# An attention and Fourier-mixing kernel on one Trainium2 core: sine table taken in during the first loads, last 64 rows in two column halves, a new instruction order

## The chip, the cores and the metric

The kernel runs on one core of a Trainium2 chip. The core has a matrix engine (TensorE, in the profile PE, its weight loads PEld), a vector engine (VectorE, DVE), an engine for activation functions (ScalarE, ACT), a general engine (GpSimd, POOL), a fifth that here only issues transfers (SyncE, SP), and 16 DMA engines that carry out all transfers. Each engine works through its own instructions strictly in order; semaphores hold an instruction back until what it needs is there. SP, ACT and POOL each issue transfers from their own queue. The metric is the time of one execution on the device in microseconds (us), lower is better; the median of several runs counts.

## What is computed

`B, H, S, D = 8, 8, 576, 64`; features `F = 128`; `C = H*D = 512`; hidden width 2048. Cut to what matters:

```python
def phi(x):
    proj = einsum('bhsd,df->bhsf', x, w_phi)
    proj = proj - max(abs(proj), axis=-1)
    return concatenate([exp(proj), exp(-proj)], -1)
q_p, k_p = phi(q), phi(k)
num = einsum('bhsf,bhfd->bhsd', q_p, einsum('bhsf,bhsd->bhfd', k_p, v))
den = einsum('bhsf,bhf->bhs', q_p, sum(k_p, axis=2))[..., None] + 1e-06
x = num / den                        # (batch, seq, 512) after merging the heads
u = x + real(fft(fft(x, axis=seq), axis=channel))
un = (u - mean(u)) / sqrt(var(u) + 1e-06)
out = u + maximum(un @ w_ch1, 0) @ w_ch2
```

## The kernel before

The eight batches pass one after the other through the same chain, and several batches are in flight at once. Rows of a batch are cut into five tiles, called c = 0 to 4: four of 128 rows and c = 4 with the last 64 (rows 257 to 319 and row 0). For the first batch everything is loaded as float32 by SP's queue and turned by TensorE (`turn_first_k`, `turn_first_q`, line 346); later batches are loaded in bfloat16 by POOL's queue (line 256) and turned by DMA transposes on SP's queue (lines 380 to 394).

The steps of one batch, with the names of their PSUM tiles:

- keys `psk` (line 464, two halves of the four, `pj` pool of two buffers): ScalarE takes two exponentials of each (470), VectorE the maximum (484, `MK`); queries `psq` (520, maximum 528) and `psh`, `ph` (570, 549, exponentials 579, 554). The maxima give factors by which POOL scales v (`VCn`, `VCp`, lines 434 and 439) and `E` (536 to 543).
- heads: `kv` (660, 664, copied by ScalarE 668), `pn_` (675, combined by VectorE 682 to 689 and POOL 690 into `X`).
- mixing: the Fourier transform as matrix products with cosine and sine tables `CS, SS, CD, SD`: folds (622 to 636), `psD` (736), then three products `pu` (757), t = 0 and 1 each giving two row tiles and t = 2 giving c = 4; VectorE adds them to `X` (762 to 772).
- normalise: statistics and centring per row tile (785 to 794) in the order c = 0, 2, 1, 3, 4, each followed by a DMA transpose on SP's queue into `UT` (798).
- forward: `psf` (844, `UT` columns 0 to 287 first, which come from c = 0, 1, 2, then the others), ReLU by ScalarE (849), `pso` (856, for c = 4 line 871), added to `X` by VectorE (862, for c = 4 line 878), and stores on SP's queue (`store`, 816 to 825).

The tables are made once: VectorE reduces the arguments (167 to 213), ScalarE takes four sines (187, 193, 212, 216), POOL clears pads and mirrors halves (231 to 249). ScalarE needs a function table loaded for sine and another for the exponential; the compiler puts these loads (`ACT_TABLE_LOAD`) ahead of the first instruction that needs them.

What sets the order: the kernel is written as generators, one per step stream, and four strings of letters (`START`, `FIRST`, `PERIOD`, `LAST`) say which stream takes its next step. `weave` follows them, delaying a letter whose needs (`NEEDS`) or PSUM buffers (`TILES`) are not there. `PERIOD` is run five times. So the strings fix each engine's instruction order. The letter Z issues one matmul of `keep_warm` (831, tile `pz`), whose result nobody reads; there are 80. The `pz` tiles come from the same three `pb` buffers as `pst`, `psq`, `kv` of the first batch, `psf` and `pso`.

The end of the program: the last batch has nothing beside it. TensorE runs 128 matmuls of `psf`, 64 of `pso` and 16 of line 871; VectorE adds the two 64-row halves of the partial sum (878, twice); SP stores 63 rows (824) and row 0 (825).

Of the kernel before, what the change touches and what calls it, by code (L numbers as in the profile page):

```python
# [9 lines left out]
AT = mybir.ActivationFunctionType  # L10
ALU = mybir.AluOpType
AX = mybir.AxisListType
F32 = mybir.dt.float32
# [8 lines left out]
FIRST = "PTTTPMFFFMFTFPQMPTPTNFMFFFMFMTFFMTSPMRKTFFPFTMFFMTFFMTFMFFMFFFFPFMRMFBFFMFAFSFFSRTSFFFFFDTFFRFPTDFFRTFFMFFATFFNMFFMMFTPVMMTTNTFTFFFFFPFFTTFFPMFTFFPTTSFFPNNN"  # L22
PERIOD = "NFKFNMFFMFMFMFMFMRFMFMMMRFFFMFFMFMFFFPPFSFRFMFFFMTFPBMPFFFNPTFFDFFFFFTRFDPQTFFFTFFMFFTFMFPTFMMFTFVRFTMFFFFMFTTTFTSFFFSFFFFFNTSTFFSTFFNTTANM"
LAST = "TPMFFTFMFTFMFMFMFMSFMFMTFNNMMFFSMFTFMFFNFFMRFFMFFMFFMFTFFTDFTFPPFFRFSFFTFTTFFFRFFFDMTFRFSFMFMTRFSMMRMFMFRFFMFMFFFDTTMPPFTMMFFPFMATFNFKBFTKFFFMMFTFFTFFMFFFFFFFNFTFNMFBNMFFFFFTFTFTFPFPPTSFNFAFFMSFTFFTFTNMFMFQFFMFTFMFRMVFFMFFFTFTSNFFFFMTDFFTFMPFFSPMFSFRNFPFNFQFTFFFFFMVRFFFPTTFMFFP"

# [7 lines left out]
def kernel(  # L33
# [23 lines left out]
    const = ctx.enter_context(tc.tile_pool(name="const", bufs=1))  # L57
# [24 lines left out]
    W2b = const.tile([128, NHH, C], BF16, name="W2b")  # L82
# [29 lines left out]
    rc, rs = gc[:, 0:C], ga[:, 3 * NK:4 * NK]  # L112
# [187 lines left out]
    def load_first():  # L300
# [509 lines left out]
        yield  # L810


    def store(b, U, c):
        if c == 1:
            for a in range(8):
                nc.sync.dma_start(
                    out=out[b, 225 - 32 * a:257 - 32 * a, :].rearrange("(r j) n -> r j n", j=2),
                    in_=U[16 * a:16 * a + 16, 0:2, 0:C],
                )
        elif c in (2, 3):  # L820
            rows_ = out[b, 320:576, :].rearrange("(a r j) n -> a r j n", r=16, j=2)
            nc.sync.dma_start(out=rows_[:, ::-1, 3 - c, :], in_=U[:, c, 0:C])
        elif c == 4:
            nc.sync.dma_start(out=out[b, 257:320, :], in_=U[1:64, 4, 0:C])
            nc.sync.dma_start(out=out[b, 0:1, :], in_=U[0:1, 4, 0:C])


    def keep_warm(b):
# [8 lines left out]
    def forward(b):  # L837
        U, UT, rs = mixed[b]
        HT = fpool.tile([128, NHH, S], BF16, tag="HT", name="HT")
        for hf in range(2):  # L840
            for hh in range(NHH):
                ps = pb.tile([128, 288], F32, tag="pb", name="psf")
                for cc in range(NCC):
                    nc.tensor.matmul(  # L844
                        ps[:], lhsT=W1b[:, cc, 128 * hh:128 * hh + 128],
                        rhs=UT[:, cc, 288 * hf:288 * hf + 288],
                        start=(cc == 0), stop=(cc == NCC - 1),
                    )
# [19 lines left out]
        po = pb.tile([128, C], F32, tag="pb", name="pso")  # L868
        for hh in range(NHH):
            g = 64 * (hh % 2)  # L870
            nc.tensor.matmul(
                po[g:g + 64, :], lhsT=HT[:, hh, 512:576], rhs=W2b[:, hh, :],
                start=(hh < 2), stop=(hh >= NHH - 2),
            )
            if hh % 4 == 3 and hh < NHH - 1:
                yield
        for g in (0, 64):
            nc.vector.scalar_tensor_tensor(
                out=U[0:64, 4, 0:C], in0=po[g:g + 64, :], scalar=rs[0:64, 4:5],
                in1=U[0:64, 4, 0:C], op0=ALU.mult, op1=ALU.add,  # L880
            )
        store(b, U, 4)
        yield

# [43 lines left out]
    def fold_later(b):  # L928
# [64 lines left out]
        "F": lambda b, i: (  # L993
            [("pb", "F", i)] if i < 32
            else [("pb", "F", i + 7)] if i < 64 and i % 8 == 0
            else [("pb", "F", i + 3)] if i == 64 else []
        ),
    }
    BUFS = {"pj": 2, "pk": 1, "pb": 3}
# [75 lines left out]
```

## Time and profile before

| | us |
|---|---|
| median of 5 runs (444.71 to 448.17) | 446.13 |
| the profiled execution | 448.01 |
| its span, first to last instruction | 445.9 |
| TensorE busy | 413.3 |
| VectorE busy | 316.0 |
| ScalarE busy | 298.8 |
| GpSimd busy | 263.1 |

The profiled execution lies 2.1 us above its span, and its time is 1.9 us above the median of the runs. The five repeats of `PERIOD` can be seen in the chain of waits: it passes the same matmuls at 231.65, 279.54 and 327.43 us, so one repeat takes 47.89 us. In the tables of stretches a row gives, for each engine, busy us and in brackets the number of instructions, then the clock that TensorE was granted (1 is full) and the mean busy share of the DMA engines.

### The profile page before, as it was taken

Reading aid. Unit: us, or ns where it says so; the run is one execution under the profiler, and the core shown is the slowest. Engines: PE = TensorE matmul, PEld = TensorE weight load, DVE = VectorE, ACT = ScalarE, POOL = GpSimd, SP = SyncE. Lnnn points to the kernel's source line nnn. Section 1 sums busy time; section 2 is a strip of 40 time slices with the busy share of each in tenths; the row PEclk is TensorE's granted clock in tenths of the full one; section 3 lists DMA queues with packets and bytes.
Section 4 is the critical chain, followed back from the end, with each engine's and each line's share of the span. In section 5 each row is a group of like instructions: output and inputs, shape, how many; then the busy total and the mean of one; then the engine's idle time right before and its main releaser. Section 6 shows DMA issues by size and latency. Waiting matters only on the chain.

```text
span 445.9 us, 10240 instructions
## 1 busy us (share of the span) xinstructions
PE 413.3 (93%) x4021; PEld 254.5 (57%) x4044; DVE 316.0 (71%) x599; ACT 298.8 (67%) x617; POOL 263.1 (59%) x363
## 2 busy tenths in 40 slices
PE   3887888999997999999999999999999999999995
PEld 2454335864475655865477546855586548745742
DVE  7968876488955979496958885897868794658012
ACT  4983568877763779677776778677967787622810
POOL 2896939494945836884487729792788156901000
PEclk9988798999998999999999999999999999999999
DMA  8996997749497396919596958857691452015004
GB/s 215 173 191 76 196 146 81 108 54 131 84 126 91 29 108 124 142 27 108 90 150 82 85 94 137 115 51 96 136 136 18 62 101 49 1 21 114 27 8 99
DMA packets 111088, 43.28 MB, mean 97 GB/s; under 512 B 85313, under 2 KB 105921, under 8 KB 111041
## 3 DMA queue, kind: packets, MB, share of 16 engines
q0 software_dynamic: 45936, 16.60, 33.1%
q1 hardware_dynamic: 64945, 25.97, 33.0%
q8 instruction: 32, 0.52, 0.5%
q14 instruction: 15, 0.12, 0.1%
q10 hardware_dynamic: 160, 0.07, 0.1%
HBM read 36.77 MB, written 9.44 MB: 104 GB/s over the span
## 4 chain that ended last, share of the span: by engine, by line
PE 69%; DVE 12%; ACT 10%; DMA 3%; POOL 3%; issue 2%; SPq 1%; ACTq 0%; DVEq 0%
PE psf L844 25%; PE pso L856 22%; PE kv L660 3%; PE pu L757 3%; PE psD L736 3%; ACT QPHN L579 2%; ACT QPHP L579 2%; PE psq L520 2%; DVE MQ L528 2%; DVE cb L687 2%; DMA UT<-UN 2%; DVE tg L682 2%; PE psk L464 2%; PE pz L831 1%; DVE MK L484 1%
## 5 line engine op out<-in xcount | busy, mean ns | idle before, releaser
L844 PE MATMUL psf<-UT,W1b 128*128 128x288 bf16 x1024 | 147.9, 289 | 3.9 <-DMA UT<-UN 2.6
L849 ACT ACTIVATE HT<-psf 128x288 bf16<-128x288 f32 x256 | 103.9, 417 | 59.3 <-PE psf L844 50.5
L856 PE MATMUL pso<-W2b,HT 128*128 128x512 bf16 x492 | 119.7, 379 | 1.6 <-issue 0.8
L844 PEld LDWEIGHTS <-W1b 128*128 128x128 bf16 x1024 | 93.4, 99 | 28.5 <-issue 2.9
L856 PEld LDWEIGHTS <-HT 128*128 128x128 bf16 x512 | 48.0, 98 | 54.3 <-issue 2.7
L690 POOL TENSOR_TENSOR X<-cb,rd 128x320 f32<-128x320 f32 x64 | 46.2, 729 | 34.3 <-DVE rd L689 33.6
L862 DVE SCALAR_TENSOR_TENSOR X<-pso,rs,X 128x512 f32<-128x512 f32 x32 | 23.4, 746 | 36.8 <-PE pso L856 36.8
L622 POOL TENSOR_TENSOR FEO<-X 128x320 f32<-128x320 f32 x59 | 48.0, 835 | 2.2
L439 POOL TENSOR_TENSOR VCn<-VS,VCn 128x512 bf16<-128x512 bf16 x28 | 31.8, 1134 | 27.4 <-issue 27.3
L528 DVE TENSOR_REDUCE MQ<-psq 128x8 f32<-128x1024 f32 (+1 forms) x40 | 39.1, 1004 | 11.4 <-PE psq L520 11.4
L470 ACT ACTIVATE KPn<-psk 128x1024 bf16<-128x1024 f32 x32 | 32.8, 1026 | 15.7 <-DVE MK L484 15.7
L484 DVE TENSOR_REDUCE MK<-psk 128x8 f32<-128x1024 f32 x32 | 38.9, 1219 | 5.7 <-ACT KPp L470 4.7
L579 ACT ACTIVATE QPHP<-psh 128x1024 bf16<-128x1024 f32 x32 | 33.0, 1030 | 12.0 <-PE psh L570 12.0
L424 POOL TENSOR_TENSOR V4N<-VS,V4N 64x256 bf16<-64x256 bf16 x14 | 8.6, 616 | 48.4 <-ACT V4N L420 47.9
L470 ACT ACTIVATE KPp<-psk 128x1024 bf16<-128x1024 f32 x32 | 32.8, 1025 | 6.5 <-PE psk L464 6.4
L579 ACT ACTIVATE QPHN<-psh 128x1024 bf16<-128x1024 f32 x32 | 33.0, 1033 | 0.0
L439 POOL TENSOR_TENSOR VCp<-VS,VCp 128x512 bf16<-128x512 bf16 x28 | 29.9, 1066 | 0.0
L785 DVE BATCH_NORM_STATS2 st<-X 128x6 f32<-128x512 f32 (+1 forms) x40 | 27.3, 683 | 0.2
L675 PEld LDWEIGHTS <-QPHP 128*128 128x128 bf16 x320 | 23.6, 99 | 4.4 <-DVE cb L687 3.3
L831 PE MATMUL pz<-wphi 128*128 128x512 bf16 x80 | 25.3, 431 | 0.6 <-ACT wphi L355 0.2
L675 PEld LDWEIGHTS <-QPHN 128*128 128x128 bf16 x320 | 22.2, 97 | 3.1 <-issue 2.0
L256 POOL DMA_DIRECT2D QS<-in_q_dram x28 | 23.1, 831 | 0.0
(410 smaller groups left out, 741.0 us busy)
## 6 DMA issues: line engine op xcount, KB each, us to landing
out_dram<-X SPq DMA_DIRECT2D x64, 64.0 KB
out_dram<-X SPq DMA_DIRECT2D x16, 256.0 KB
KS<-in_k_dram POOLq DMA_DIRECT2D x14, 256.0 KB, 5.3
QS<-in_q_dram POOLq DMA_DIRECT2D x14, 256.0 KB, 4.9
VS<-in_v_dram POOLq DMA_DIRECT2D x7, 512.0 KB, 6.3
W1b<-in_moe_w_ch_dram POOLq DMA_DIRECT2D x1, 2048.0 KB, 17.3
W2b<-in_moe_w_ch_dram POOLq DMA_DIRECT2D x1, 2048.0 KB, 15.4
W2b<-in_k_dram SPq DMA_DIRECT2D x2, 512.0 KB
```

The costliest lines, as they stand in the source:

```text
L439: nc.gpsimd.tensor_tensor(out=VC[:, hs, :, 0:D], in0=values[b][0][:, hs, :].rearrange("p h (j d) -> p h j d", d=D), in1=VC[:, hs, :, D:D + ...
L470: nc.scalar.activation(out=KP[:, hs, :, :].rearrange("p e (jp jj) f -> p jj (e jp) f", jj=2), in_=psk[:], func=AT.Exp, scale=sgn,)
L484: nc.vector.tensor_reduce(out=MK[:, 2 * pr:2 * pr + 2, :].rearrange("p e (jp jj) -> p jj (e jp)", jj=2), in_=tiles[pr][:], axis=AX.X, op=A ...
L528: nc.vector.tensor_reduce(out=o, in_=i[:], axis=AX.X, op=ALU.max, apply_absolute_value=True)
L579: nc.scalar.activation(out=o, in_=psh[:], func=AT.Exp, scale=sgn)
L622: eng.tensor_tensor(out=FEO[:, :, i, a:a + D], in0=X[:, :, a:a + D], in1=X[:, :, C - a:C - a - D:-1], op=op,)
L675: nc.tensor.matmul(pn_[:, i, 65 * c:65 * c + 65], lhsT=QP[:, h, 128 * c:128 * c + 128], rhs=kvh[:, i, :], start=True, stop=True,)
L690: nc.gpsimd.tensor_tensor(out=X[:, :, D * h:D * h + D], in0=cb[:, :, 0:D], in1=rd[:].to_broadcast([128, 5, D]), op=ALU.mult,)
L831: nc.tensor.matmul(pz[:].rearrange("p (a n) -> p a n", n=DF), lhsT=wphi2[:], rhs=wphi2[:].unsqueeze(1).to_broadcast([128, C // DF, DF]), s ...
L844: nc.tensor.matmul(ps[:], lhsT=W1b[:, cc, 128 * hh:128 * hh + 128], rhs=UT[:, cc, 288 * hf:288 * hf + 288], start=(cc == 0), stop=(cc == N ...
L849: nc.scalar.activation(out=HT[:, hh, 288 * hf:288 * hf + 288], in_=ps[:], func=AT.Relu)
L856: nc.tensor.matmul(po[:], lhsT=HT[:, hh, 128 * c:128 * c + 128], rhs=W2b[:, hh, :], start=(hh == 0), stop=(hh == NHH - 1),)
```

## The change

It has three parts.

1. A new `activation` of one column (`sined`, never read) with the sine function follows the two transfers that ScalarE's queue issues first. The compiler now puts the load of the sine table ahead of it, and no load ahead of the copy of line 355 or ahead of line 187. Two loads are left (sine, exponential) where there were three.
2. For the last batch, the c = 4 step of `forward` is done in two halves of 256 columns: 32 matmuls of 256 columns in place of 16 of 512, four additions of 64x256 in place of two of 64x512, two stores of 63 rows x 1 KB on SP's queue in place of one of 63 x 2 KB, and two of row 0, now on ScalarE's queue. Other batches keep the one step. `TILES` is told of the second `pb` buffer.
3. All four strings are new. The number of each engine's other instructions stays the same. What moves on the engines:
   - Start, TensorE: the transposes of the first keys and queries come in one run of 12 and one of 8 in place of 4, 8, 4 and 4, with two `pz` between them where there were seven; but behind the next group of four there are 14 `pz` ahead of the third `psk`, where there were 11. The fourth `psk` and the last query transposes keep their neighbourhood; kv of heads 0 to 4 is spread between `psh`, `psq` and `pt`. POOL's issue of the W2b load comes one step of line 690 earlier.
   - Entry to the first `forward`: TensorE had 12 `pz`, `psq`, two `psh` tiles, `psq`, `kv`, then 12 `psf`. Now it has 15 `pz`, `psq`, `kv`, one `psh` tile, 4 `psf`, and the second `psh` tile behind the third head's `kv`. POOL issues the second query load after all eight steps of line 439 in place of after four.
   - First batches: SP's queue stores c = 4 of batch 0 ahead of three query transposes in place of behind them.
   - `PERIOD`: `pt` (536) and ScalarE's `E` come later, the two `psh` tiles of line 570 come ahead of the second `pu` in place of behind it, and 16 + 2 `pso` matmuls lie between the first and the second `pu` where there were 8. On VectorE the additions of line 862 move by a few steps. On SP's queue the store of c = 2 comes ahead of the third `UT` transpose (c = 1) in place of behind it.

```diff
-START = "GZZZCGZSCZZGGSZJCTZTZZCSTJKTPDWTGRSZZZSZZZZZZZTZRRTPZTZZSRTJTZMSMRTZPTTZSJPJMMMTPSTTCMBMMMRMZZZRTPZTTMWNZMATTTMZMMZZZZPMQZMNMZZZMZSZZMZZZZZZZTZZZZZZZZMZDTNTZZRNZVMZTZZZQZMZZZZZZRZTZZNRNZZZ"
+START = "GZSZZCGCGJZTZCSGJTPTCTZKGZZWZTRZZZZSZSZZRZZRZZJTTPRZZTTZZZZZSJMTZRZBZSMMTNTSDPNPJMTCZTPMTMMMMZZMTRWZTPTZMZTMTZANZTMMMZTMMZPQZMZZZZZMZZZZMZZZZZZTZZRZDMZZSSTZRVZTZMZMTZZTZZZNRZZZZZNSRZQNZZZZ"
...
-PERIOD = "NFKFNMFFMFMFMFMFMRFMFMMMRFFFMFFMFMFFFPPFSFRFMFFFMTFPBMPFFFNPTFFDFFFFFTRFDPQTFFFTFFMFFTFMFPTFMMFTFVRFTMFFFFMFTTTFTSFFFSFFFFFNTSTFFSTFFNTTANM"
+PERIOD = "SFSKMFFMFMFMFMNFMSNFMFMMMFFAMFFMFFMFFFPPFFFMTFFMFBPFFNMFFPTRPFFFFFFRDFTFDPRTFTRMFFTFFFFFMFFFRTMFQMTFMFTFVFFFFFFTTTTFPMFNFFFFTTFFFFFTSTSMTNN"
...
     nc.vector.memset(halfpi[:], float(np.pi / 2))
+    sined = const.tile([128, 1], F32, name="sined")
...
             nc.scalar.dma_start(out=wphi_f[64 * e:64 * e + 64, :], in_=w_phi[:, :])
+
+        nc.scalar.activation(out=sined[:], in_=halfpi[:], func=AT.Sin)
...
-    def store(b, U, c):
+    def store(b, U, c, cols=slice(0, C)):
...
-            nc.sync.dma_start(out=out[b, 257:320, :], in_=U[1:64, 4, 0:C])
-            nc.sync.dma_start(out=out[b, 0:1, :], in_=U[0:1, 4, 0:C])
+            nc.sync.dma_start(out=out[b, 257:320, cols], in_=U[1:64, 4, cols])
+            first = nc.scalar if b == B - 1 else nc.sync
+            first.dma_start(out=out[b, 0:1, cols], in_=U[0:1, 4, cols])
...
+        halves = 2 if b == B - 1 else 1
+        for half in range(halves):
+            cols = slice(C // halves * half, C // halves * (half + 1))
+            po = pb.tile([128, C], F32, tag="pb", name="pso")
+            for hh in range(NHH):
+                g = 64 * (hh % 2)
+                nc.tensor.matmul(
+                    po[g:g + 64, cols], lhsT=HT[:, hh, 512:576], rhs=W2b[:, hh, cols],
+                    start=(hh < 2), stop=(hh >= NHH - 2),
+                )
+                if (hh + 1) % (4 * halves) == 0 and hh < NHH - 1:
+                    yield
+            for g in (0, 64):
+                nc.vector.scalar_tensor_tensor(
+                    out=U[0:64, 4, cols], in0=po[g:g + 64, cols], scalar=rs[0:64, 4:5],
+                    in1=U[0:64, 4, cols], op0=ALU.mult, op1=ALU.add,
+                )
+            store(b, U, 4, cols)
+            yield
```

More of the change, by code (lines that the diff above doesn't have):

```diff
@@ L18 @@
 MAGIC = 12582912.0
-START = "GZZZCGZSCZZGGSZJCTZTZZCSTJKTPDWTGRSZZZSZZZZZZZTZRRTPZTZZSRTJTZMSMRTZPTTZSJPJMMMTPSTTCMBMMMRMZZZRTPZTTMWNZMATTTMZMMZZZZPMQZMNMZZZMZSZZMZZZZZZZTZZZZZZZZMZDTNTZZRNZVMZTZZZQZMZZZZZZRZTZZNRNZZZ"
-FIRST = "PTTTPMFFFMFTFPQMPTPTNFMFFFMFMTFFMTSPMRKTFFPFTMFFMTFFMTFMFFMFFFFPFMRMFBFFMFAFSFFSRTSFFFFFDTFFRFPTDFFRTFFMFFATFFNMFFMMFTPVMMTTNTFTFFFFFPFFTTFFPMFTFFPTTSFFPNNN"
-PERIOD = "NFKFNMFFMFMFMFMFMRFMFMMMRFFFMFFMFMFFFPPFSFRFMFFFMTFPBMPFFFNPTFFDFFFFFTRFDPQTFFFTFFMFFTFMFPTFMMFTFVRFTMFFFFMFTTTFTSFFFSFFFFFNTSTFFSTFFNTTANM"
-LAST = "TPMFFTFMFTFMFMFMFMSFMFMTFNNMMFFSMFTFMFFNFFMRFFMFFMFFMFTFFTDFTFPPFFRFSFFTFTTFFFRFFFDMTFRFSFMFMTRFSMMRMFMFRFFMFMFFFDTTMPPFTMMFFPFMATFNFKBFTKFFFMMFTFFTFFMFFFFFFFNFTFNMFBNMFFFFFTFTFTFPFPPTSFNFAFFMSFTFFTFTNMFMFQFFMFTFMFRMVFFMFFFTFTSNFFFFMTDFFTFMPFFSPMFSFRNFPFNFQFTFFFFFMVRFFFPTTFMFFP"
+START = "GZSZZCGCGJZTZCSGJTPTCTZKGZZWZTRZZZZSZSZZRZZRZZJTTPRZZTTZZZZZSJMTZRZBZSMMTNTSDPNPJMTCZTPMTMMMMZZMTRWZTPTZMZTMTZANZTMMMZTMMZPQZMZZZZZMZZZZMZZZZZZTZZRZDMZZSSTZRVZTZMZMTZZTZZZNRZZZZZNSRZQNZZZZ"
+FIRST = "RPMTFSMFRFMTPTMKPTFFMTTBSPPFMFFFMTTNPMFTFFPFMMFSFTFFMFQFFFMFFTMMFFFFTMFMFNPRFAFRFFTFFFDFFFFTFFPTRFDFFTFFMFFSFFMTFMMSFPMFTTMTTFTFPFFVFFFTFNFFTTPFFMPTAFFPTNNN"
+PERIOD = "SFSKMFFMFMFMFMNFMSNFMFMMMFFAMFFMFFMFFFPPFFFMTFFMFBPFFNMFFPTRPFFFFFFRDFTFDPRTFTRMFFTFFFFFMFFFRTMFQMTFMFTFVFFFFFFTTTTFPMFNFFFFTTFFFFFTSTSMTNN"
+LAST = "NNTFMFRFFMFMFMPTFMFRMTFMFMMTTMPFFMFTFTFMFFMTFNTFMFFMSFFTFFPFFFKFFMDRFFMFBFFFFTFFFFFTPPFDSFFFTFMRMMMMAMMMSFMMFFMTFMFFFTTMFFFFFMFTPFFTFRTFFFFFFNRFFMRFSPFTFMMFAFTTBMFFTNFFPMDFFFFVSPRVFSFMFFFFMFPRFKFFSPTFFTFFFFFQFMTPDFTTFFNFFTFFFNMSFMTFRFFFQFPFMMFTFNSFMNFFFTFMFFMFPFFNFFTSTTTNFFFFFN"
 @with_exitstack
@@ L867, in forward @@
             yield
[L868 to L883, printed above, removed]
+        halves = 2 if b == B - 1 else 1
[17 more added lines that the diff above has]
+            yield
     staged, parts = {}, {}
@@ L995 @@
             else [("pb", "F", i + 7)] if i < 64 and i % 8 == 0
-            else [("pb", "F", i + 3)] if i == 64 else []
+            else [("pb", "F", i + (1 if b == B - 1 else 3))] if i == 64 or i == 66 and b == B - 1
+            else []
         ),
```

## The prediction

> **What bounds the kernel.** I read the page's busy rows and slices first, then a table of stretches.
>
> ```profile
> PE 413.3 (93%) x4021; PEld 254.5 (57%) x4044; DVE 316.0 (71%) x599; ACT 298.8 (67%) x617; POOL 263.1 (59%) x363
> ...
> PE   3887888999997999999999999999999999999995
> ...
> PEclk9988798999998999999999999999999999999999
> ```
>
> ```profile
> core 0: us, PE busy (x) PEld busy (x) DVE busy (x) ACT busy (x) POOL busy (x), PEclk, DMA share, GB/s
> 0.00:44.00 44.00, 30.63 (x349) 19.26 (x351) 34.31 (x70) 28.90 (x51) 29.93 (x64) 0.94 0.89 164
> 44.00:96.00 52.00, 45.88 (x458) 28.35 (x455) 35.75 (x75) 38.29 (x81) 36.95 (x48) 0.92 0.96 127
> ...
> 135.00:183.00 48.00, 44.66 (x428) 26.72 (x430) 34.24 (x62) 33.53 (x70) 29.90 (x38) 0.96 0.66 90
> ...
> 279.00:327.00 48.00, 47.27 (x497) 29.62 (x497) 37.25 (x69) 35.99 (x77) 32.70 (x44) 1.00 0.70 100
> ```
>
> In a repeat of PERIOD (279 to 327) TensorE is busy 47.27 of 48 us at full clock: it is the bound, its matmuls don't change, and a new order can save at most 0.7 us there, but can lose more. The room is elsewhere: 13.4 us idle before 44, 6.1 to 96, 3.3 from 135 to 183, and about 5.3 behind the last matmul (440.5 to 445.9).
>
> **Table loads.** The timeline of ScalarE (start, us, operation, idle before it):
>
> ```profile
> 6.14 1.28 ACT L355 ACT_TABLE_LOAD   x1 [6.14 <-DMA wphi_f<-in_w_phi_dram]
> 7.44 0.30 ACT L355 CAST wphi<-wphi_f 128x128 bf16<-128x128 f32 x1
> 7.64 0.37 ACT L348 CAST KT<-pst 128x256 bf16<-128x256 f32 x1
> 8.03 1.28 ACT L187 ACT_TABLE_LOAD   x1
> 9.32 1.00 ACT L187 ACTIVATE SS<-gs 128x960 bf16<-128x960 f32 x1
> ...
> 12.94 1.28 ACT L455 ACT_TABLE_LOAD   x1
> ```
>
> ScalarE issues two transfers until 1.93 us and then waits for w_phi until 6.14. The new sine load (1.28) and the one-column sine (0.2, from the smallest ACT rows) fit in 1.93 to 3.4: free; they would cost 1.5 only if w_phi landed by 2. The load at 6.14 goes, but the KT copy behind it waits for transposes that end at 7.56 anyway, so it saves only the wphi copy's lateness. The load at 8.03 does stand in the way: its arguments are ready at 6.42. So all from line 187 to the first exponential moves up by 1.28: sines end at 11.66, K4p starts at 12.95. The Trainium skill, "ScalarE: Activation LUTs", section "What ACT_TABLE_LOAD costs", charges about 2.66 us per switch, load plus a drain. By it 2.7 would be won; the rows show 1.28 with the copy ending at 8.01 and the sine starting at 9.32, no drain. I take 1.28.
>
> How much reaches the end? Four rows of the start:
>
> ```profile
> 14.16 1.52 DVE L225 TENSOR_SCALAR TURN<-tn,blk 128x128 f32<-128x128 f32 x1
> 15.38 0.22 POOL L161 MEMSET ET<- 128x128 bf16 x1
> 17.33 2.97 PE L831 MATMUL pz<-wphi 128*128 128x512 bf16 x11
> 20.25 0.40 PE L464 MATMUL psk<-wphi,KT 64*128 64x128 bf16 x8
> ```
>
> The first TURN takes 1.52 and ends at 15.68, just after POOL's last pad memset (15.60); its twin behind it takes 0.28. I read that as VectorE held by POOL's memsets. These follow the sines, so they end at 14.3 in the new kernel, 1.28 earlier. VectorE then has one copy more (0.65) in front of the maxima, so MK moves up only about 0.5. TensorE then meets 14 pz where it had 11: at 0.26 each (2.97 less the last one's length, over ten) that is 3.65 from about 17.3, so the third psk goes at about 21.4, not 20.25. In the old kernel the 11 pz ended just as MK freed the buffer (20.17): hidden; three more are not. Against that, kv of the last heads no longer waits behind the queries and POOL's VC chain starts 0.6 earlier (21.6 for 22.25), so the combine chain (33.78, VectorE from there without a gap to 45) starts between 0.4 and 1.3 earlier. Ends: +0.5 and -1.3; I take **-0.6**, since the chain runs through both.
>
> **Entry to the first forward.** TensorE stands idle 1.12 at 66.87 and 1.80 at 69.06, both times psh waiting for VectorE's MK, 0.17 at 69.66, and the first 12 psf run cold (70.71 to 73.5). The new order sends psq, one kv and one psh, then psf; the second psh no longer blocks them. UT limits it: its third transpose is issued near 66.6. From the last batch (issued 411.31, DMA engines quiet by 414.1) a transpose takes 2.8 to land: 69.4 against 70.7. So -1.3 from that, or up to -3.1 if the idle goes wholly, 0 if VectorE (full from 58 to 71) delays psq as before. I take **-1.5**. The three extra pz fall into this idle time. POOL's W2b issue (1.21) moves into its idle 36.97 to 39.06: nothing, because the chain waits for VectorE by 43.91. The later query load is used only 30 us on.
>
> **Batches 0 and 1.** TensorE waits 2.6 for UT at 135.6 to 138.2, then runs 12 psf in 3.04 for 1.47: 4.2 lost. SP's three query transposes (122.81 to 128.35) stood ahead of the two UT transposes; they still do, and the stores now wait ahead of them for line 878 (end 124.6). I expect UT neither earlier nor much later: 0 (between -4.2 and +1.3).
>
> **PERIOD.** Nothing to win but 0.2 at 320.79: 0. The price is under the rivals.
>
> **The tail.** By TensorE and VectorE alone the halves help. Rows: 16 matmuls of line 871 take 1.87, two additions 1.53.
>
> ```profile
> 440.58 1.53 DVE L878 SCALAR_TENSOR_TENSOR X<-pso,rs,X 64x512 f32<-64x512 f32 x2 [1.10 <-PE pso L871]
> 442.14 0.29 SPq L824 DMA_DIRECT2D out_dram<-X  x1
> ...
> 441.50:442.00 0.50, 0.00 (x0) 0.00 (x0) 0.50 (x1) 0.00 (x0) 0.00 (x0) 1.00 0.53 188
> ...
> 443.50:444.00 0.50, 0.00 (x0) 0.00 (x0) 0.00 (x0) 0.00 (x0) 0.00 (x0) 1.00 0.56 209
> ```
>
> Half the columns at half the time is 0.94 per half; weight loads allow it, as kv's 65-column matmuls come every 31 to 33 ns with a load each. An addition of 256 columns is 0.45 (0.15 for one column, 0.75 for 512). So the halves end at 439.6 and 440.55, the last addition at 441.5, not 442.11. A rule speaks against it: "TensorE: Matmul & The Clock Gate", section "Back-to-back issue gap", gives about 81 ns per matmul of 128 columns with its load. That makes 1.3 per half and 442.2 at the end: no gain. I take the row. Row 0 on ScalarE's queue saves SP one issue, 0.34. Together the last issue would be 0.9 earlier. But the last two lines above show the output flowing at about 200 GB/s (last column) from 441.5 to 444.3 without a gap: the stores of c = 2, 3 and 4, 640 KB, leave one behind the other, and c = 4 would wait for c = 3 until about 443.6 even if issued earlier. The drain sets the end: 128 KB more at 195 GB/s ends at 444.3, not 444.4. Ends: -0.9 (queue free) and +0.6 (126 packets of 1 KB at the rate of 2 KB ones, 98 per us). I take **-0.2**, by the row of the drain.
>
> **Sum.** -0.6 - 1.5 + 0 + 0 - 0.2 = -2.3. Profiled: span 445.9 to 443.6, execution 448.0 to 445.7. Against the median of 446.13: **443.8 us**. What can be told from no change is 0.5%, 2.2 us; the forecast lies on that edge.
>
> **Rivals.**
> - B, the start gives nothing: pz and TURN eat the load's gain, psq still waits for VectorE. For it: VectorE full from 58 to 71 and the three pz. Only the tail's 0.2 is left: 445.9. Chance 0.17.
> - C, the stall at 135 goes as well, because the pipeline arrives with UT in time: -2.3 - 4.2 = -6.5, 439.6. For it: the old UT took 7.2 us to land (131.06 to 138.22) against 2.8 when quiet, so a little less crowding is enough. Against: SP's order gets no better. 0.22.
> - D, slower: in PERIOD, UT of c = 1 becomes late. From the end of the second pu to the first psf there were 8.5 us (310.1 to 318.64); the new order takes 8 pso (1.7) and four psh (0.7) out, leaving 6.1. VectorE needs 2.7 from pu to UN of c = 1 (762, 765, 768, 785, 786, 794), so the transpose is issued 3.4 before psf. It was 3.86 before. With 2.8 to land, the slack falls from 1.06 to 0.6. If landing takes 1.75 longer under load (4.55; far less than the 7.2 seen), psf stands 1.15 in each of five repeats: +5.75 - 2.3 = +3.45, 449.6. It is slower by over 0.5% from 0.9 per repeat, landing at 4.3. Everything in TensorE's order stands behind that psf. 0.19.
>
> The forecast itself has 0.42, with its own range 442.5 to 445.1.
>
> **How the numbers follow.** Faster: half of the forecast's chance and a bit (0.23), C 0.22, the edge of B 0.04: 0.49. Slower: D but its edge 0.18. Same: 0.33. The range cuts the lower half of C (0.09) and the upper half of D (0.10): 440.0 to 449.0, wide because C's stall and D's wait are both unknown.
>
> **What would show it.** ScalarE: a sine load near 1.9, none at 6 or 8, K4p near 13. TensorE: third psk near 21.4 and combine from 33; first psf near 69.2; a repeat still 47.9 (longer, with psf waiting for UT, is D); the wait near 136 there (C if gone). Tail: additions end near 441.5 while the last bytes still leave at 444. It is wrong if psf starts later than 70.7, or if the repeats change by more than 0.2.

## The result and the profile after

The changed kernel takes 444.95 us (median of 28 runs, 441.72 to 450.88) against 446.13 for the kernel before, run beside it (47 runs). The ratio is 0.9959, with a 95% interval from 0.9938 to 0.998: some 1.8 us less, of which the interval leaves between 0.9 and 2.8. The ratio is one of means, without the runs (4 of 28, 3 of 47) that lie more than 1.5% above the fastest of their kernel; the two medians, over all runs, are 1.2 us apart. The forecast was 443.8, 0.5% less. The profiled execution took 446.34 us with a span of 444.4 (before: 448.01 and 445.9).

The first lines of the page of the changed kernel: busy time of TensorE and the others, then TensorE's busy tenths and its granted clock in 40 slices.

```profile
PE 409.8 (92%) x4036; PEld 252.6 (57%) x4060; DVE 315.4 (71%) x601; ACT 298.0 (67%) x617; POOL 263.5 (59%) x363
...
PE   3886887999998999899989999999999989999994
...
PEclk9998899999999999999999999999999999999998
```

TensorE's share hardly moves. Its granted clock dips once, in slices 4 and 5 (0.53 from 41.8 to 49.1 us); the old kernel has this dip and three more, at 0.50 from 25.2 to 28.6, from 69.6 to 73.0 and from 137.9 to 141.3. In the slices (11.1 us each) the 7 of the old kernel at slice 13, the wait near 135, has become an 8; but 8s appear at slices 17, 21 and 33, where the old row was all 9s. The table of stretches of the changed kernel says where (us, busy us and count of each engine, clock, DMA share, GB/s):

```profile
core 0: us, PE busy (x) PEld busy (x) DVE busy (x) ACT busy (x) POOL busy (x), PEclk, DMA share, GB/s
0.00:44.00 44.00, 30.70 (x355) 19.48 (x355) 35.98 (x72) 28.75 (x53) 30.97 (x65) 0.97 1.05 180
44.00:96.00 52.00, 46.10 (x468) 28.61 (x471) 36.71 (x76) 38.90 (x82) 38.19 (x50) 0.96 0.90 114
...
135.00:183.00 48.00, 47.03 (x487) 29.27 (x490) 36.19 (x67) 35.87 (x75) 31.04 (x41) 1.00 0.75 97
183.00:231.00 48.00, 46.28 (x480) 28.85 (x484) 36.09 (x67) 35.35 (x75) 31.77 (x42) 1.00 0.74 100
231.00:279.00 48.00, 46.02 (x480) 28.39 (x480) 36.05 (x67) 35.48 (x74) 32.23 (x42) 1.00 0.74 97
279.00:327.00 48.00, 47.21 (x490) 29.40 (x492) 37.18 (x70) 36.40 (x76) 32.90 (x43) 1.00 0.79 102
```

From 183 to 279 the old kernel had TensorE busy 47.26 of every 48 us, here in the first half of that stretch:

```profile
183.00:231.00 48.00, 47.26 (x497) 29.62 (x497) 37.24 (x69) 35.98 (x76) 32.69 (x43) 1.00 0.73 100
```

Now it is 46.28 and 46.02: about a microsecond more is lost in each of two repeats of `PERIOD`, which the forecast had put at nothing.

A busy share doesn't say how far the kernel has come. For that I take one step that both kernels run once per batch, the first matmul of the c = 4 step of `forward` (line 871 before, 879 after), from the timeline of TensorE. Under the two kernels stand four of the experiments below.

| batch | 0 | 1 | 2 | 3 | 4 | 5 | 6 | 7 | span |
|---|---|---|---|---|---|---|---|---|---|
| before | 119.50 | 171.92 | 219.81 | 267.71 | 315.59 | 363.48 | 406.47 | 438.62 | 445.9 |
| after | 116.27 | 167.20 | 216.26 | 265.27 | 312.47 | 360.36 | 404.55 | 436.70 | 444.4 |
| lead of after | 3.23 | 4.72 | 3.55 | 2.44 | 3.12 | 3.12 | 1.92 | 1.92 | 1.5 |
| `sine_alone` | 118.14 | 170.34 | 218.23 | 266.13 | 314.02 | 361.91 | 404.90 | 437.06 | 444.9 |
| `new_front` | 117.44 | 172.20 | 220.09 | 267.99 | 315.88 | 363.77 | 406.76 | 438.92 | 446.1 |
| `k_split` | 117.25 | 165.68 | 213.40 | 260.60 | 307.79 | 355.57 | 398.57 | 430.72 | 438.5 |
| `best2` | 117.26 | 166.26 | 213.45 | 260.65 | 307.84 | 356.07 | 398.91 | 431.05 | 438.4 |

So the change wins 4.7 us up to batch 1 and gives 3.2 of them back, net: 2.3 in the next two repeats (49.06 and 49.01 us in place of 47.89), 1.2 in batch 6 and 0.4 in the tail, with 0.7 won in between (a repeat of 47.20). Each row of the table is one execution, and the front varies from one to the next: with the same `START` and `FIRST` as the changed kernel, batch 0 comes at 115.96 in `tail_old` and at 120.00 in `best2_actq`, two of the experiments below.

The longest waits of TensorE in the changed kernel (us in total, times, longest):

```profile
PE psf L848 <- DMA UT<-UN: 4.9, 4, 2.4
PE psf L848 <- DMA KT<-KS: 1.7, 1, 1.7
...
PE psf L848 <- DVE X L775: 1.0, 1, 1.0
```

By place, given as the start of the wait, they are: 2.40 at 133.0 (in the kernel before 2.60 at 135.6), 1.75 at 182.7, 1.7 at 231.8, 0.52 at 315.7 and 1.03 at 363.6. The second and third lines are named wrongly, and a reader should know how to see it. `psf` doesn't read `KT`; that transpose stands right behind the one of `UT` on the same queue. Nor does `psf` need the addition of line 775: in `k_split`, which has the same order there, TensorE starts this `psf` ahead of VectorE's addition.

```profile
358.63 0.65 PE L848 MATMUL psf<-UT,W1b 128*128 128x288 bf16 x4
```

```profile
359.10 0.68 DVE L775 TENSOR_TENSOR X<-pu,X 64x512 f32<-64x512 f32 x1
```

What is left for both is `UT`, the only other thing that these `psf` read and that was in flight.

Here is the wait at 182.7, in three timelines of the changed kernel: SP's queue, POOL's queue, and TensorE (start, us, operation, idle before it).

```profile
171.45 1.24 SPq L395 DMA_TRANSPOSE QT<-QS  x1
172.80 3.13 SPq L396 DMA_TRANSPOSE QT<-QS  x1
176.03 1.19 SPq L397 DMA_TRANSPOSE QT<-QS  x1
177.31 1.20 SPq L801 DMA_TRANSPOSE UT<-UN  x1
```

```profile
175.59 2.30 POOL L257 DMA_DIRECT2D KS<-in_k_dram  x3
```

```profile
184.45 1.15 PE L848 MATMUL psf<-UT,W1b 128*128 128x288 bf16 x8 [1.75 <-DMA UT<-UN]
```

`UN` of c = 4 was ready at 173.08 (line 797). Its transpose stands behind three query transposes on SP's queue and is issued at 177.31, when POOL has already put a megabyte of keys for a later batch (three issues from 175.59) on the DMA engines. It lands after 7.14 us, if `psf` starts as it lands. Two repeats on, at 274.16, the same transpose is issued 0.50 behind the first key issue instead of 1.72, and nobody waits. In the kernel before it was 0.22 to 0.48 in three repeats; here is the second of them, POOL's queue and then SP's:

```profile
229.62 2.32 POOL L256 DMA_DIRECT2D KS<-in_k_dram  x3
```

```profile
229.84 1.21 SPq L798 DMA_TRANSPOSE UT<-UN  x1
```

Two things set this lead of the keys. Counted from the c = 4 step of the table, POOL now issues them 8.4 us behind instead of 9.8, in every repeat. And the last `UT` waits on SP's queue until the three query transposes are issued, which takes 5.8 and 5.5 us (from 171.45 and 220.51) where it comes late and 4.5 (from 269.53) where it doesn't.

### The profile page after: what moved, and what is told of

Its sections match the earlier page's. It is cut to its first block, busy times and chain, and to the rows that moved or that the text cites. A ratio compares the mean times of both kernels' runs of the same rounds, so it can differ in the third digit from the quotient of the medians.

```text
span 444.4 us, 10274 instructions
## 1 busy us (share of the span) xinstructions
PE 409.8 (92%) x4036; PEld 252.6 (57%) x4060; DVE 315.4 (71%) x601; ACT 298.0 (67%) x617; POOL 263.5 (59%) x363
## 4 chain that ended last, share of the span: by engine, by line
PE 71%; DVE 11%; DMA 8%; ACT 5%; POOL 2%; issue 2%; SPq 0%; DVEq 0%; ACTq 0%; POOLq 0%
PE psf L848 25%; PE pso L860 24%; DMA UT<-UN 4%; PE pu L760 3%; PE psD L739 3%; PE kv L663 3%; PE pso L879 2%; DVE MK L487 2%; PE psq L523 2%; PE psk L467 2%; DMA HT<-in_k_dram 1%; DMA KT<-KS 1%; ACT QPHN L582 1%; ACT QPHP L582 1%; DVE X L886 1%
## 5 line engine op out<-in xcount | busy, mean ns | idle before, releaser
L848 PE MATMUL psf<-UT,W1b 128*128 128x288 bf16 x1024 | 146.2, 286 | 9.1 <-DMA UT<-UN 4.9
L848 PEld LDWEIGHTS <-W1b 128*128 128x128 bf16 x1024 | 91.9, 98 | 34.0 <-issue 8.2
L442 POOL TENSOR_TENSOR VCn<-VS,VCn 128x512 bf16<-128x512 bf16 x28 | 30.2, 1077 | 12.8 <-ACT VCn L437 12.3
L442 POOL TENSOR_TENSOR VCp<-VS,VCp 128x512 bf16<-128x512 bf16 x28 | 31.5, 1126 | 0.0
L835 PE MATMUL pz<-wphi 128*128 128x512 bf16 x80 | 24.3, 420 | 0.6 <-ACT kvh L671 0.3
```

Source lines behind the costliest of these rows:

```text
L442: nc.gpsimd.tensor_tensor(out=VC[:, hs, :, 0:D], in0=values[b][0][:, hs, :].rearrange("p h (j d) -> p h j d", d=D), in1=VC[:, hs, :, D:D + ...
L848: nc.tensor.matmul(ps[:], lhsT=W1b[:, cc, 128 * hh:128 * hh + 128], rhs=UT[:, cc, 288 * hf:288 * hf + 288], start=(cc == 0), stop=(cc == N ...
```

## The experiments

Every kernel was timed in five rounds beside the kernel before; ratios are to it, with 95% intervals. Its own median was 447.08 beside the first four, 446.71 beside `k_split`, `k_split_old`, `tail_old` and `best1`, and 445.95 beside the rest, so times of different groups are compared by their ratios. Theory 1 is that the new front wins, and that the bytes of the keys, issued ahead of the last `UT`, make it late and take most of the gain back.

### What the front is worth

**`sine_alone`**: the kernel before with the one-column sine alone.

```diff
+        nc.scalar.activation(out=sined[:], in_=halfpi[:], func=AT.Sin)
```

> The kernel before, with nothing but the one-column sine behind the w_phi transfers; orders and tail are the old ones. Theory 1 (the table load is a small part of the gain): K4p starts near 12.95 to 13.1 instead of 14.23, the combine chain between 0.4 and 1.3 us earlier, and with nothing else changed -0.3 to -1.1 us in the time, ratio 0.9975 to 0.9993. Rival (VectorE, full from 58 to 71, swallows it before the first forward): first psf still at 70.7 and the time within 0.2 us of the kernel before.

446.6 us, ratio 0.9978 (0.9955 to 1.0001). The first exponential K4p starts at 13.01, the combine chain at 32.48 instead of 33.78, the first `psf` at 69.39 instead of 70.71, and the lead at the last c = 4 step is 1.56. The rival falls: in this execution VectorE swallows nothing of the 1.3 us. The time itself can't be told from none at this precision, though only just.

**`new_front`**: the kernel before with the sine and the new `START` and `FIRST`.

```diff
-START = "GZZZCGZSCZZGGSZJ
...
+START = "GZSZZCGCGJZTZCSG
...
-FIRST = "PTTTPMFFFMFTFPQM
...
+FIRST = "RPMTFSMFRFMTPTMK
...
```

> The kernel before with the one-column sine and the new START and FIRST; PERIOD, LAST and the tail are the old ones. Theory 1 (the new front wins about 4 us, the new PERIOD and LAST give over 2 of them back through a late UT of c = 4): first psf near 66, the lead of 3 to 4 us is still there at the end, 442.0 to 443.0, ratio near 0.992, and a repeat of 47.9 us without waits of psf for UT behind the first one near 133. Rival (the lead can't be kept whatever the PERIOD, because the transfers set the pace): the waits for UT come with the old PERIOD too, and the time is that of the changed kernel, 444.5 to 445.5.

446.96 us, ratio 0.9981 (0.9954 to 1.0008). Neither theory holds as a whole: the repeats are without waits for `UT`, as theory 1 said, but the lead is not kept; the rival's time is within the interval, but not for its reason, since the waits in the repeats don't come. The first `psf` comes at 65.94 and the c = 4 step of batch 0 leads by 2.06, but at that of batch 1 the lead is gone (172.20 against 171.92). After it every repeat takes 47.89. Most of the loss is one wait, and what follows it; TensorE's timeline of `new_front`:

```profile
137.29 3.04 PE L847 MATMUL psf<-UT,W1b 128*128 128x288 bf16 x12 [3.31 <-DMA UT<-UN]
141.23 2.53 PE L847 MATMUL psf<-UT,W1b 128*128 128x288 bf16 x12
```

Twelve such matmuls take 1.64 at full clock. The wait of 3.31 costs 5.6 us in all: 3.31, then 1.40 and 0.89 of slow matmuls. In the kernel before it was 2.60 and 1.40. So in this execution the earlier front buys nothing, because `UT` comes late there: TensorE arrives sooner and waits longer. The granted clock, 0.50 from 137 to 143, adds to it; the run of 448.08 that was profiled is one of those with a low clock (last section).

### Why UT is late

**`k_late`**: the changed kernel; all three key issues of a repeat behind the first line 693.

```diff
-PERIOD = "SFSKMFFMFMFMFMNFMSNFMFMMMFFA
...
+PERIOD = "SFSMFFMFMFMFMNFMSNFMFMMKMFFA
...
```

> The changed kernel, with POOL's load of the next keys (three issues) moved behind the first line 693 of the same repeat; SP's queue is untouched. Theory 1 (UT of c = 4 lands late because 1 MB of keys issued 1.5 to 1.7 us ahead of it goes first through the DMA engines): KS is now issued some 3 us behind UT instead of ahead of it, UT lands in under 5 us instead of 7.1, the waits of 1.75 at 182.7 and 1.7 at 231.8 go, the one of 2.4 near 133 falls below 1; 440.0 to 442.5, ratio to the changed kernel near 0.992. Rival (it is the three query transposes ahead of UT on SP's queue): the waits stay over 1.3 each and the time is that of the changed kernel within 0.5 us, 444.5 to 445.5.

449.38 us, ratio 1.0059 (1.0039 to 1.008): slower than both, so neither theory's time came. At the three places the waits for `UT` are gone, as theory 1 says: the query transposes, which stand where they stood, were not enough to cause them, unless the waits hide under a new one, which `k_split` tests. The place I chose has a price, which the waits and the timeline of TensorE in `k_late` show:

```profile
PE psq L523 <- DVE cb L690: 7.3, 10, 0.8
```

```profile
183.41 0.40 PE L523 MATMUL psq<-wphi,QT 64*128 64x128 bf16 x8 [0.66 <-DVE cb L690]
184.61 0.40 PE L523 MATMUL psq<-wphi,QT 64*128 64x128 bf16 x8 [0.80 <-DVE cb L690]
```

POOL's three issues take 2.31 us, and POOL frees the buffers of `cb` (line 693). VectorE waits for these, and TensorE for VectorE: 1.46 in each repeat, which then takes 48.84.

**`ut_first`**: the changed kernel; the last `UT` transposes ahead of the query transposes on SP's queue (the letter A goes behind the N).

```diff
-FIRST = "RPMT ... TTPFFMPTAFFPTNNN"
+FIRST = "RPMT ... TTPFFMPTFFPTNNNA"
-PERIOD = "SFSKMFFMFMFMFMNFMSNFMFMMMFFAM ... TSTSMTNN"
+PERIOD = "SFSKMFFMFMFMFMNFMSNFMFMMMFFM ... TSTSMTNNA"
```

> The changed kernel, with the last UT transposes of a batch ahead of the three query transposes on SP's queue, and nothing else. Theory 1 and its first rival both expect the waits of psf for UT to go (UT of c = 4 is issued when its UN is ready, near 173.1 instead of 177.3): 440.0 to 442.5. Second rival (the lost time only moves, because the query transposes are then late for psq, or VectorE sets the pace): psf no longer waits but psq does, by 1 us or more per repeat, and the time stays at 444.5 to 445.5.

447.33 us, ratio 0.9984 (0.9956 to 1.0012). In the repeats it does what it should: 47.19 and 47.20 for the first two, with `UT` issued 2.49 us ahead of the keys. In the first batches the second rival is right. TensorE's timeline of `ut_first`:

```profile
137.34 0.60 PE L523 MATMUL psq<-wphi,QT 64*128 64x128 bf16 x8 [2.79 <-DMA QT<-QS]
137.88 3.06 PE L848 MATMUL psf<-UT,W1b 128*128 128x288 bf16 x12
```

What is issued together with the keys is late, whichever transpose it is: there the queries were issued from 126.78, the keys from 126.83. From batch 0 to batch 1 it takes 54.16, where the changed kernel took 50.93.

**`k_split`**: the changed kernel; only the third of the key issues (512 KB read, nearly half of the bytes) moved as in `k_late`, a third of the delay for POOL. `K` now takes two letters, so it is doubled in all four strings.

```diff
-        load(pieces, range(3))
+        load(pieces, range(2))
+        yield
+        load(pieces, range(2, 3))
         yield
...
-PERIOD = "SFSKMFFMFMFMFMNFMSNFMFMMMFFA
...
+PERIOD = "SFSKMFFMFMFMFMNFMSNFMFMMKMFFA
...
```

> The changed kernel, with only the third of POOL's three key issues (512 KB read) moved behind the first line 693; the first two stay where they are. The delay of POOL at that place is a third of that in the run before (0.77 us instead of 2.31), so VectorE's cb should not wait. Theory 1 (the bytes of the keys ahead of UT make it late): the waits of psf for UT near 133, 182.7 and 231.8, in all 5.85 us in the changed kernel, fall to under 1.5 in all, and no wait of psq for cb comes; 440.0 to 442.5. Rival (with the keys moved, UT was as late as ever, and only hidden under the 1.5 us that psq waited for cb): psf waits over 1 us at two or more of the three places, and the time is 444.5 to 445.5.

441.44 us (six runs, 440.44 to 441.84), ratio 0.9888 (0.9849 to 0.9927). The waits for `UT` sum to 0.6, no `psq` waits for `cb`, and repeats take 47.72, 47.20, 47.19 and 47.78. POOL, SP and TensorE in `k_split` at the place shown above:

```profile
174.07 1.57 POOL L257 DMA_DIRECT2D KS<-in_k_dram  x2
...
178.82 0.82 POOL L257 DMA_DIRECT2D KS<-in_k_dram  x1
```

```profile
175.79 1.20 SPq L801 DMA_TRANSPOSE UT<-UN  x1
```

```profile
181.59 1.15 PE L848 MATMUL psf<-UT,W1b 128*128 128x288 bf16 x8 [0.41 <-DMA UT<-UN]
```

The keys again lead `UT` by 1.72 us, SP's queue takes as long over the query transposes, and only the bytes ahead are nearly halved: `UT` lands after 5.80 instead of 7.14. That settles it for this place and these two executions. The transposes on SP's queue and the loads on POOL's are carried by the same engines, as the Trainium skill has it ("DMA: Bandwidth & Descriptors", section "Issuing engines are not separate DMA queues": all run on the same 16 DMA engines and interleave); these two rows put the price at 1.3 us for 512 KB read, an estimate from one pair.

**`k_split_old`**: the same edit in the kernel before (K behind the same M of its `PERIOD`).

```diff
-PERIOD = "NFKFNMFFMFMFMFMFMRFMFMMMRFFF
...
+PERIOD = "NFKFNMFFMFMFMFMFMRFMFMMKMRFFF
...
```

> The kernel before, with the third key issue of each repeat moved behind line 690 in the same way and nothing else. Theory 1: the wait of 2.6 us for UT at 135.6 falls below 1, and with it the slow psf behind it (3.04 us for 12 where 1.64 is normal) goes; the other repeats, which had no wait, stay at 47.9: 2 to 4 us less than the kernel before, ratio 0.991 to 0.996. Rival (in the old order UT is late because SP's queue issues it behind the query transposes and the stores): the wait stays over 2 and the ratio is within 0.9975 to 1.0025.

444.85 us, ratio 0.996 (0.9937 to 0.9983). The wait falls from 2.60 to 1.22, above the 1 expected, and the slow matmuls behind it are gone (12 in 1.63). From batch 0 to batch 1 it takes 49.63 instead of 52.42; the other repeats stay at 47.89. This one edit is worth to the old kernel what the whole change was, 0.4%.

### The tail

I measure it in the trace, from the first matmul of the last c = 4 step to the span's end; 0.4 us is below what the timing resolves.

**`tail_old`**: the changed kernel with the old tail.

```diff
-            first = nc.scalar if b == B - 1 else nc.sync
-            first.dma_start(out=out[b, 0:1, cols], in_=U[0:1, 4, cols])
+            nc.sync.dma_start(out=out[b, 0:1, cols], in_=U[0:1, 4, cols])
...
-        halves = 2 if b == B - 1 else 1
+        halves = 1
```

> The changed kernel with the old tail: c = 4 of the last batch in one piece, row 0 on SP's queue. Theory 1 (the halves give no gain: the end is set by the drain of the output and by what closes the program, and two queues with 1 KB packets make both longer): from the first matmul of the last c = 4 step to the span's end 7.2 to 7.8 us instead of 7.7 to 9.0 with the new tail, of which 1.5 instead of 1.9 lies behind the last byte; 0 to 1.0 us less than the changed kernel. Rival (the forecast's -0.2 or more is there): 0.2 to 0.9 us more than the changed kernel.

445.04 us, ratio 0.9939 (0.991 to 0.9967), not to be told from the changed kernel's 0.9959. The tail takes 7.17. Over all kernels: with the old tail 7.28 (before), 7.84, 7.18, 7.29, 7.17, 7.08, 7.35 and 7.38; with the new one 7.70 (after), 8.96, 8.62 and 7.78. The new tail does not pay. (The spans are rounded to 0.1, so each of these can be off by 0.05.)

This run holds a second lesson. Up to the tail its order is that of the changed kernel, yet its profiled execution (441.72) has no wait at 182 or 231 and three repeats of 47.19 to 47.20; its 22 runs go from 440.29 to 449.37. In these repeats SP's queue is through with the query transposes in 4.6 to 5.0 us, and the keys lead `UT` by 0.53 to 0.94. So whether `UT` is in time differs between executions of one order, by about a microsecond on SP's queue; why the query transposes take longer in one of them is not shown. `k_split`, which gives `UT` room, stays within 1.4 us in its six runs.

**`best2_halves`** and **`best2_actq`**: the kernel `best2` (below), with the halves alone and with row 0 on ScalarE's queue alone.

```diff
-        halves = 1
+        halves = 2 if b == B - 1 else 1
```

```diff
-            nc.sync.dma_start(out=out[b, 0:1, cols], in_=U[0:1, 4, cols])
+            first = nc.scalar if b == B - 1 else nc.sync
+            first.dma_start(out=out[b, 0:1, cols], in_=U[0:1, 4, cols])
```

> The kernel best2 with c = 4 of the last batch in two column halves, row 0 still on SP's queue (four stores on one queue). Theory 1 (1 KB packets and two more issues lengthen the drain): from the first matmul of the last c = 4 step to the span's end 7.5 to 8.5 us, against 7.1 to 7.3 in best2, with 1.5 behind the last byte. Rival (the halves are free or gain, and it is ScalarE's queue that lengthens the end): 6.8 to 7.3.

> The kernel best2 with row 0 of the last batch stored by ScalarE's queue, c = 4 in one piece. Theory 1 (a second queue at the end makes the closing of the program longer by 0.35, and saves one issue on SP): from the first matmul of the last c = 4 step to the span's end 7.3 to 7.7 us against 7.1 to 7.3 in best2, with 1.85 behind the last byte instead of 1.5. Rival (the queue saves its issue of 0.34 and costs nothing): 6.8 to 7.2.

440.52 us, ratio 0.9868 (0.983 to 0.9907), tail 7.46; and 440.76, ratio 0.9877 (0.9836 to 0.9918), tail 7.08. For the queue alone the rival held; for the halves 7.46 lies between the two expectations. Neither part alone stands out from the old tails, and behind the last packet of output lie 1.3 to 1.4 us in each, as with the old tail. Only the two together are long, which I had not foreseen. What is different then is in the issues. The store of 63 rows on SP's queue in the changed kernel (ns, lowest, median, highest of nine), and ScalarE's two issues of row 0 beside it:

```profile
L827 SPq DMA_DIRECT2D out_dram<-X x9: 292/313/783, 121.7 to 439.9; - x9
```

```profile
438.84 1.25 ACTq L829 DMA_DIRECT2D out_dram<-X  x2
```

The last store takes 783 ns to issue while ScalarE issues too, and 732, 854 and 1791 ns in the other three kernels with both parts; with the halves on SP's queue alone it took 390. The first of the two stores, which ScalarE's queue accompanies as well, takes only 292 in the changed kernel. The last packet of output ends 1.7 us before the end in three of the four kernels and 2.0 in `k_late`, not 1.4; in `k_late` and `ut_first`, which have the longest tails, it also comes a microsecond later (7.0 behind the first matmul instead of about 6.0). The longer issue is in all four; that it makes the longer tail is argued, not shown.

### Put together

**`best1`**: `k_split` with the old tail and the old `LAST`. **`best2`**: `best1` with `UT` first in the repeats, but not in the first batches.

```diff
-PERIOD = "SFSKMFFMFMFMFMNFMSNFMFMMKMFFA ... TSTSMTNN"
+PERIOD = "SFSKMFFMFMFMFMNFMSNFMFMMKMFF ... TSTSMTNNA"
```

> The changed kernel with the third key issue moved as above, the old tail, and the LAST of the kernel before. Theory 1: the three gains add up: about -4 from UT, -0.5 from the tail, -1.0 from psf no longer waiting at 363.6 for X of line 775: 438.5 to 440.5, ratio to the kernel before 0.982 to 0.987. Rival (what is won at UT is lost again where VectorE or the transfers set the pace): 443 to 445.

> The fast version so far (third key issue late, old tail, old LAST), and in the repeats, but not in the first batches, UT of c = 4 ahead of the query transposes on SP's queue. Theory 1: the 2.2 us that psf still waited for UT, in four places, fall below 1 and no wait of psq for the query transposes comes, since in the repeats they have time: 438.5 to 440.0, ratio 0.981 to 0.986. Rival (the query transposes are then late, as they were by 2.8 us in the first batches with UT first): psq waits over 1 us per repeat, 442 to 445.

`best1`: 440.69 us, ratio 0.9863 (0.9819 to 0.9908); psf waits 2.2 for `UT` in four places. `best2`: 440.55 us, 0.9867 (0.9831 to 0.9903); 0.9 in one place, and no wait for queries. Both beat the kernel before by 1.3% and the changed kernel by nearly 1%. The 0.8 us by which they lie below `k_split` are within the intervals, so what the old tail and the old `LAST` add is not shown; nor is, in the time, what `UT` first adds to `best1`. `best1` is within the range that was expected of it, `best2` half a microsecond above its own. Of the three gains that I expected of `best1` the third was read from the wrongly named wait above.

**`best2_nosine`**: `best2` without the one-column sine.

```diff
-        nc.scalar.activation(out=sined[:], in_=halfpi[:], func=AT.Sin)
```

> The kernel best2 without the one-column sine; everything else is the same. Theory 1 (the table load's 1.28 us reach the end almost whole where no wait for UT swallows them): combine chain from 33 instead of near 32, and 0.7 to 1.3 us more than best2. Rival (VectorE and the first loads hide it): within 0.3 us of best2.

442.57 us, ratio 0.9913 (0.9888 to 0.9939): 2.0 us more than `best2` by the medians (the intervals just overlap), above the 1.3 expected; in the traces the last c = 4 step is 3.67 later (434.72). The combine chain starts at 34.68 instead of 31.93, 2.75 later. That is more than a table load, and the rest is TensorE's clock. K4p is 1.34 later (14.49 for 13.15). VectorE's copy of the keys is then late too, TensorE waits 1.69 for it instead of 0.88, and its granted clock falls to half behind that wait. The same stretch in `best2`, `best2_nosine` and `best2_actq`, in the columns of the table of stretches above (the clock is the third number from the right):

```profile
16.50:20.00 3.50, 3.44 (x19) 1.74 (x18) 3.50 (x6) 2.80 (x7) 2.06 (x4) 1.00 1.17 136
```

```profile
16.50:20.00 3.50, 2.95 (x22) 1.91 (x22) 2.57 (x5) 2.85 (x3) 2.54 (x4) 0.57 0.76 73
```

```profile
16.50:20.00 3.50, 3.50 (x12) 1.43 (x11) 3.46 (x5) 2.15 (x6) 1.98 (x4) 0.53 1.22 141
```

In `best2_actq`, which has the sine (K4p at 12.81), a wait of 1.81 at the same place was followed by the same dip, and its combine chain starts at 33.14, 1.21 later than in `best2`. So about half of the 2.75 comes with a dip that can happen without the late table load; whether the late load makes it more frequent isn't shown.

## Why the forecast held, and which of its steps did not

The total was right to 1.2 us (443.8 against 444.95), by errors that cancelled, and that is luck. By its own last sign, "if the repeats change by more than 0.2", the account behind the total is wrong: they take 49.06, 49.01 and 47.20 us. Term by term, against the profiled execution:

- **Table load, right in its mechanism.** The new load is at 1.95, none at 6 or 8, the sine of line 188 at 8.10 and K4p at 13.11 (forecast 12.95). ScalarE's timeline of the changed kernel:

```profile
1.95 1.28 ACT L319 ACT_TABLE_LOAD   x1 [1.95 <-issue]
3.25 0.20 ACT L319 ACTIVATE sined<-halfpi 128x1 f32<-128x1 f32 x1
...
8.10 1.01 ACT L188 ACTIVATE SS<-gs 128x960 bf16<-128x960 f32 x1
...
11.82 1.28 ACT L458 ACT_TABLE_LOAD   x1
```

  The row's 1.28 was the right price of a load; of a drain beside it, by which 2.7 would have been won, nothing shows. The size of the term, -0.6, was too small: alone it moved the combine chain by 1.30 and the last c = 4 step by 1.56. I had let VectorE and the three pz eat half of it.
- **The three pz**, "at 0.26 each": they take 0.22, and the third `psk` goes at 20.32, not 21.4. Four rows of the start of the changed kernel, to set beside those of the forecast:

```profile
12.31 2.14 DVE L226 TENSOR_SCALAR TURN<-tn,blk 128x128 f32<-128x128 f32 x1
...
14.56 0.29 DVE L226 TENSOR_SCALAR TURN<-tn,blk 128x128 f32<-128x128 f32 x1
...
17.03 3.24 PE L835 MATMUL pz<-wphi 128*128 128x512 bf16 x14
...
20.32 0.23 PE L467 MATMUL psk<-wphi,KT 64*128 64x128 bf16 x1
```

  TURN waits again until POOL's last memset ends (14.37), as I had read it. The combine chain starts at 31.89, 1.89 earlier, beyond the 1.3 that I gave as the upper end.
- **Entry to the first forward**, -1.5 and first `psf` at 69.2: it came at 66.09, but four of them only; the next eight wait 1.62 for `kv` and run from 68.67. The third `UT` transpose, which was to hold `psf` until 69.4, is issued at 63.54; the 66.6 that I counted from is where its issue ended in the old kernel. Counting the columns of all matmuls but pz, the amount of work that the old kernel has done at 79.93 is done at about 77.9. So start and entry together gave 2.0 where I had 2.1: right in sum, too little for the first and too much for the second. But this is one execution. With the same `START` and `FIRST` the same amount is done at 77.4 in `tail_old`, 78.7 in `k_split`, 79.0 in `new_front` and 81.4 in `best2_actq`; `sine_alone`, with the old entry, has 78.6. Part of it is the clock behind one and the same wait of 1.62. TensorE's rows, and the stretches from 68 to 71, of the changed kernel and of `k_split`:

```profile
68.67 1.14 PE L848 MATMUL psf<-UT,W1b 128*128 128x288 bf16 x8
68.00:71.00 3.00, 2.64 (x47) 1.95 (x47) 1.40 (x3) 3.00 (x10) 2.83 (x3) 1.00 0.20 25
```

```profile
68.60 2.11 PE L848 MATMUL psf<-UT,W1b 128*128 128x288 bf16 x8
68.00:71.00 3.00, 2.92 (x27) 2.22 (x27) 0.70 (x2) 2.06 (x6) 3.00 (x4) 0.50 0.17 24
```

  So what the entry alone is worth isn't shown.
- **Batches 0 and 1**, "0 (between -4.2 and +1.3)": from c = 4 of batch 0 to that of batch 1 it took 50.93 instead of 52.42, a gain of 1.5. The wait was nearly as long, but the clock held behind it, so 1.40 of slow matmuls went (12 take 1.64 at full clock, not the 1.47 of the forecast, so the old stall had cost 4.0, not 4.2). Before, then after:

```profile
138.36 3.04 PE L844 MATMUL psf<-UT,W1b 128*128 128x288 bf16 x12 [2.60 <-DMA UT<-UN]
```

```profile
135.40 1.14 PE L848 MATMUL psf<-UT,W1b 128*128 128x288 bf16 x8 [2.40 <-DMA UT<-UN]
```

  As far as these executions show, that too is luck and not the order. In `new_front`, `sine_alone` and `ut_first`, with waits of the same kind, it didn't hold.
- **PERIOD**, "Nothing to win but 0.2: 0": this is the step that failed, in both directions. A repeat without waits takes 47.20, not 47.89, so all of the 0.7 that I called the most it could save is saved, where nothing waits. And the last `UT` came late in two of the repeats, 1.75 and 1.7 us, because POOL reached the key load 1.4 us sooner, and so more of that load came ahead of it. From batch 1 to batch 5 that makes +1.6 where `k_split`, the same order with the keys split, has -1.7. I had listed SP's queue for every moved step, but not the load on POOL's queue: its letter is no earlier in the order, but half of the VCn and VCp steps that POOL does ahead of it were.
- **Rival D** named a wait that came: `UT` of c = 1, landing in about 4.5 us, makes `psf` wait 1.15, it said; at 363.6 `psf` waited 1.03 for the transpose of c = 1, issued at 360.06, and 0.52 at 315.7. But that happened twice, not in each repeat, and what cost more was its neighbour, c = 4. Most of the 1.2 us lost in batch 6 is the wait at 363.6. Rival C, that the wait near 133 goes by itself, didn't come; it took `k_split`.
- **Tail**, -0.2: the halves are ready nearly as worked out. The 32 matmuls take 1.94, 61 ns each, so the row was right and not the 81 ns that the forecast weighed against it; the additions end at 439.84, 3.14 behind the first matmul, where the old tail took 3.49 and the forecast had 2.9. And the drain decides, as said. Data leave at 180 to 203 GB/s until 442.5; these are rows of the changed kernel's stretches, the last column:

```profile
440.00:440.50 0.50, 0.00 (x0) 0.00 (x0) 0.00 (x0) 0.00 (x0) 0.00 (x0) 1.00 0.54 203
...
442.00:442.50 0.50, 0.00 (x0) 0.00 (x0) 0.00 (x0) 0.00 (x0) 0.00 (x0) 0.50 0.53 180
442.50:443.00 0.50, 0.00 (x0) 0.00 (x0) 0.00 (x0) 0.00 (x0) 0.00 (x0) 0.50 0.07 23
```

  But they end no sooner behind the first matmul than before (6.0 and 5.9), and the program ends 1.7 after them instead of 1.4: +0.4, inside the +0.6 that I had as the bad end. Two queues at once was the part that I had counted as a saving of 0.34. It saved nothing.

## What to carry to other kernels

When an order changes, look at what each queue will now issue earlier, not only at what the order moves: a prefetch that nobody needs for 17 us (keys issued at 175.6, first read by a matmul at 192.7) can slip ahead of a transfer that is needed in 5. Where a transfer lands within tenths of its use, one trace tells little, since the same program waits in one execution and not in the next; give it room by splitting or moving the bulk ahead of it, and in six runs of `k_split` the spread shrank along with the time. And a load that is moved to make room is paid on the queue that issues it: moving three issues on a busy queue cost 1.46 us per repeat, moving one of them nothing.

## What the runs showed of the hardware

- **A wait of 1.6 to 3.3 us can cost TensorE its clock, or not.** After waits near 135 of 2.29 (`sine_alone`), 2.60 (before), 2.79 (`ut_first`) and 3.31 (`new_front`), 12 matmuls took 3.04 to 3.06 instead of 1.64; after 2.40 (after) and 2.61 (`tail_old`) 8 took the full-clock 1.14. After the wait of 1.62 near 68, 8 took 1.14 (after, `tail_old`) or 2.11 (`new_front`, `k_split`), at a granted clock of 1.00 or 0.50. The length alone doesn't decide. The Trainium skill ("TensorE: Matmul & The Clock Gate", section "HAM oscillation — how this bites in real kernels") warns of gaps above some 3.4 us; here shorter ones were followed by the drop.
- **A good part of the spread from run to run goes with the clock.** Divided at a mean granted clock of 0.985, 40 runs of the kernel before average 448.4 us below it and 35 average 445.6 above; for `sine_alone` it is 447.4 (14) and 444.9 (8), for `new_front` 447.6 (15) and 444.6 (7). The changed kernel has only 4 of 28 runs below. Whether fewer dips are the gain, or come of fewer waits, these runs don't tell.
- **The second of two stores can take longer to issue while a second queue issues.** It took 0.73 to 1.79 us on SP's queue beside ScalarE's, 0.39 alone. The first, also beside ScalarE's, took 0.29 to 0.50, and 0.29 alone.
